# A per-pair scale made on all partitions by one matmul, in an attention stage whose written-out order is laid out anew

## The chip, the cores and the metric

The kernel runs on one core of a Trainium2 chip. The core has five engines that each work through their own queue of instructions in order: TensorE (PE; its weight loads are shown apart as PEld), VectorE (DVE), ScalarE (ACT), GpSimd (POOL) and SyncE (SP), which here only issues DMAs. They wait for each other by semaphores. The metric is the device time of one execution in microseconds (us), lower is better. Before the change the median of three runs is 683.49 us (682.04 to 684.49).

## The reference

Attention over 2 batches x 8 heads, sequence 1152, head dimension 64, with queries averaged in pairs (576 queries a head), followed by two MLPs:

```
q_pool = q.reshape(B, H, S//2, 2, D).mean(axis=3)
scores = q_pool @ k.T / sqrt(D);  scores -= scores.max(-1)
attn   = exp(scores);  attn = attn / (attn.sum(-1) + 1e-9)
x      = attn @ v                              # -> 1152 tokens x 512
h = x @ w_in;  g = max(h,0) + alpha*min(h,0);  x = g @ w_out          # 512 -> 2048 -> 512
h = x @ w_in2; g = P(h) / (Q(|h|) + 1e-6);     out = g @ w_out2       # P cubic, Q quadratic
```

All inputs are float32, and the kernel keeps nearly float32 accuracy by splitting operands into a high and a low part and adding up the products of the parts.

## The kernel before, in words

**Pairs.** The 16 heads are worked in 8 pairs p = 0..7; head n = 2p is the even and n = 2p+1 the odd head of a pair, 9 key tiles t a head, so a pair is 18 steps. For each step PE makes scores (`score`, L1049, four matmuls into an `st` tile), ACT exponentiates (`p_exp`, L1057, PSUM tile `st` to the tile `PF`), DVE or POOL forms the low part (`p_lo`, L1063, tile `PL`), and PE multiplies with V (`av`, L1075, L1077 and L1079, 15 matmuls into the accumulator tile `o` of the head, with the high and low part of V in `V16`). When a head's nine steps are done, `norm` (L1088 to L1090, DVE) divides `o` into the tile `x`.

**Beside that, for the next pair.** While pair p-1 runs its scores, PE, ACT and DVE also find the row maxima of pair p (`max_mm` L962, `max_relu` L968, `max_1` L971, `max_2` L976), and the operands of pair p+1 are prepared: `load_q` (tile `qr`), `load_k` (`kr` or `ring`) and `load_v` (`vr`) are DMAs from HBM; `q_sum` (L820, POOL, tile `qs`) adds the two query halves; `k_hi` and `q_hi` (ACT, L824 and L838, tiles `kh` and `qh`) round to the high parts; `k_diff` (L827, POOL), `q_lo` and `k_lo` (DVE) follow; and `k1_move`, `qh_move`, `ql_move`, `k2_move` (all recorded at L816, on SP) copy the parts by DMA into the matmul operands `K1`, `QQ` and `K2`. All DMAs of the kernel are issued from SP, in the order of its queue.

**V's scale.** V is scaled by a power of two per pair, from the largest |V|. `v_abs` (L889, ACT) sums |V| by partition into `am`, one number a partition. `v_max` (L899, PE) transposes this column: the stationary operand is the one column `am`, the moving one the identity, the output one row of 128 numbers in a free corner of the accumulator tile `o` of the even head then in work. `v_scale` (L904 to L909, DVE) takes the maximum of that row and forms the scale and its inverse, on one partition (tile `g`). `v_scale2` (L912, PE) spreads the two numbers over 128 partitions by a matmul with a row of ones, into the same corner of `o`, and `v_scale3` (L917, DVE) copies them to the tile `vs`. `v_hi` (L934, ACT) and `v_lo` (L938, DVE) use `vs`. Since `v_max` and `v_scale2` write the tile `o` and DVE reads it, the next `av` matmuls into `o` wait for DVE.

**What sets the order.** Every call is put into one list with a time in steps (`at(time, fn, ...)`; pair p starts at 18p), the list is sorted by time, and the instructions are issued in that order, so each engine's queue has the list's order. The number is no clock: an instruction runs when its queue has come to it and its semaphores are there. A table `NUDGE`, looked up by the function's name and its time (pairs 1 to 5 by the time within the pair), adds a correction to it.

**Late in attention** the weights of the first MLP are unpacked as well: five operations a tile on ACT, DVE (`w_shift` L657, `w_top` L662, `w_low` L670) and POOL. From then on the MLPs run as a stream of matmuls (L708 and L1331).

Of the kernel before, what the change touches and what calls it, by code (L numbers as in the profile page):

```python
# [21 lines left out]
P = 128  # L22

NUDGE = {
    "av +10.35": 0.124,
    "av +11.35": -0.146,
    "av +15.34": -0.123,
    "av +15.35": 0.109,
    "av +2.35": 0.223,
    "av +4.34": -0.294,  # L30
    "av +4.35": 0.851,
    "av +8.34": -0.854,
    "av +8.35": -0.053,
# [24 lines left out]
    "av 17.35": 1.881,
    "av 4.35": 0.449,
    "av 6.34": -0.922,  # L60
    "av 6.35": 0.509,
    "av 8.35": 0.307,
    "first_kd -51.10": 0.806,
    "first_kd -54.50": 0.086,
    "first_kh -52.00": -0.087,
    "first_kh -52.60": 0.123,
    "first_kh -55.31": 0.328,
    "first_kh -55.32": 0.122,
    "first_kh -55.80": -0.617,
    "first_kl -51.00": 1.543,  # L70
    "first_kl -53.40": -0.149,
    "first_m -48.09": 7.849,
    "first_qh -50.30": -0.541,
    "first_qh -51.00": -0.312,
    "first_qh -51.80": 0.273,
    "first_qh -53.50": -1.065,
    "first_qh -55.95": 0.245,
    "first_ql -51.10": 0.279,
    "first_ql -55.30": 0.085,
    "init_1 -59.90": -3.438,  # L80
    "init_2 -59.70": -0.534,
    "init_3 -48.10": 9.574,
    "k1_move +7.30": -0.198,
    "k1_move +9.10": 2.890,
    "k1_move -47.27": 5.618,
    "k1_move -47.90": 4.202,
    "k1_move 11.70": 2.488,
    "k1_move 13.50": 1.398,
    "k2_move +0.36": 2.161,
    "k2_move +11.50": 0.543,  # L90
    "k2_move 108.36": 1.833,
    "k2_move 15.90": -0.539,
    "k2_move 8.10": -0.649,
    "k2_move 8.20": 1.103,
    "k_diff +6.50": 0.474,
    "k_diff -47.90": 0.005,
    "k_diff 10.90": -0.273,
    "k_hi +5.50": 0.667,
    "k_hi -47.90": -1.004,
    "k_hi 9.90": 0.525,  # L100
    "k_lo +10.00": 0.415,
    "k_lo 14.40": -1.147,
    "k_lo 7.04": -0.214,
    "load_k +13.00": -0.638,
    "load_k -59.98": 3.729,
    "load_k -59.99": 0.074,
    "load_k 1.50": 0.485,
    "load_k 13.00": -0.200,
    "load_q +13.00": 5.133,
    "load_q -59.97": 0.305,  # L110
    "load_q -60.00": -2.525,
    "load_q 1.50": 0.105,
    "load_q 13.00": 3.721,
    "load_v +13.00": -0.984,
    "load_v -59.96": 2.431,
    "load_v 0.69": 0.463,
    "load_v 13.00": 1.710,
    "max_1 +0.83": -0.321,
    "max_1 +10.86": 0.076,
    "max_1 +12.30": 0.259,  # L120
    "max_1 +2.27": -0.100,
    "max_1 +3.70": 0.078,
    "max_1 +8.00": -0.159,
    "max_1 -49.55": 0.073,
    "max_1 -50.55": 0.080,
    "max_1 -51.55": -0.390,
    "max_1 -52.55": -0.144,
    "max_1 -53.55": 0.216,
    "max_1 0.55": -0.363,
    "max_1 10.50": -0.036,  # L130
    "max_1 108.83": -0.043,
    "max_1 111.70": -0.169,
    "max_1 113.13": 0.091,
    "max_1 114.56": 0.031,
    "max_1 116.00": 0.031,
    "max_1 117.43": 0.031,
    "max_1 118.86": 0.031,
    "max_1 12.80": 0.042,
    "max_1 120.30": -0.006,
    "max_1 15.10": 0.428,  # L140
    "max_1 16.25": 0.161,
    "max_1 4.22": -0.411,
    "max_1 5.44": 0.202,
    "max_1 7.05": -0.166,
    "max_1 8.20": -0.037,
    "max_1 9.35": -0.040,
# [1320 lines left out]
```

## Time and profile before

| | us |
|---|---|
| median of 3 runs | 683.49 (682.04 to 684.49) |
| profiled execution, its own time | 685.3 |
| span of the profiled execution | 681.8 |
| PE busy in the span | 646.8 (95%) |
| DVE busy | 515.9 (76%) |
| ACT busy | 484.5 (71%) |
| POOL busy | 402.7 (59%) |

The span runs from the first to the last instruction; the profiled execution's own time has a little more around it. Busy time is a mean over stages that have different limits, so what matters is which wait ends last in the stage in question: the list of waits names the engine and line that waited, and the one that released it; the timeline shows where it stood; and a table of stretches shows what the stage took. The granted clock (PEclk) is 1.00 or 0.50 of TensorE's full speed, 2.4 or 1.2 GHz.

### The profile page before, as it was taken

To read this page: it belongs to the slowest core of one execution; us is meant where nothing else is said; L and a number is where in the kernel's file an instruction comes from. 1 tells how busy PE (TensorE), PEld (TensorE's weight loads), DVE (VectorE), ACT (ScalarE), POOL (GpSimd) and SP (SyncE) were. 2 spreads that over 40 slices of the span, in tenths; PEclk is the share of its full clock that TensorE was granted. 3 is DMA by queue.
4 is the path that set the end of the run, shared out by engine and by line. 5 is a ranking of instruction groups with operands and counts; after the bars stand their busy time and mean duration, and the time that the engine had idled before them with its cause. 6 is when DMAs were issued, how large, how long until landed. Compare 5 with 4: busy or idle time off the path is not lost.

```text
span 681.8 us, 13647 instructions
## 1 busy us (share of the span) xinstructions
PE 646.8 (95%) x5194; PEld 580.2 (85%) x5194; DVE 515.9 (76%) x949; ACT 484.5 (71%) x902; POOL 402.7 (59%) x353
## 2 busy tenths in 40 slices
PE   6798999799998889999999999999998999999997
PEld 5677999798897879999999999999887779999995
DVE  8887666769677998998992149996788877767774
ACT  5666687577867756666764368888788888778774
POOL 5554677567676775676664226785466655444442
PEclk8799799899999979999999999999999999999999
DMA  4778759595684224343331005640320010001001
GB/s 173 192 203 176 156 137 212 119 230 122 168 196 114 68 92 154 126 140 138 128 133 49 1 0 189 232 167 32 124 92 32 1 47 1 2 0 48 1 0 46
DMA packets 20960, 72.28 MB, mean 106 GB/s; under 512 B 3104, under 2 KB 3104, under 8 KB 20896
## 3 DMA queue, kind: packets, MB, share of 16 engines
q1 hardware_dynamic: 20896, 71.42, 37.3%
q8 instruction: 40, 0.66, 0.4%
q14 instruction: 24, 0.20, 0.1%
HBM read 47.72 MB, written 2.36 MB: 73 GB/s over the span
## 4 chain that ended last, share of the span: by engine, by line
PE 61%; DVE 19%; ACT 9%; issue 5%; DMA 4%; SPq 1%; POOL 1%; POOLq 0%; DVEq 0%; ACTq 0%
PE hp L708 20%; PE acc L1331 18%; PE st L1049 9%; PE m L962 5%; DVE bits L662 3%; PE o L1075 3%; PE o L1077 2%; PE o L1079 2%; DVE bits L657 2%; DMA QQ<-qh 2%; DVE ring L670 2%; DMA QQ<-qs 1%; DVE g L1312 1%; DVE g L1297 1%; DVE hp L1310 1%
## 5 line engine op out<-in xcount | busy, mean ns | idle before, releaser
L1063 POOL TENSOR_TENSOR PL<-PF 128x576 f16<-128x576 f32 x106 | 132.5, 1262 | 65.2 <-ACT PF L1057 64.0
L1320 POOL TENSOR_TENSOR gl<-g,gh 128x384 fp32r<-128x384 f32 x96 | 104.7, 1091 | 72.2 <-ACT gh L1316 58.2
L1057 ACT ACTIVATE PF<-st 128x576 f32<-128x576 f32 x144 | 91.4, 651 | 41.4 <-PE st L1049 35.1
L1331 PE MATMUL acc<-woh,gl 128*128 128x512 f32 x288 | 114.4, 397 | 3.2 <-POOL gl L1320 3.2
L1331 PE MATMUL acc<-woh,gh 128*128 128x512 f32 x288 | 113.3, 393 | 2.1 <-ACT m L1362 1.7
L1331 PE MATMUL acc<-wol,gh 128*128 128x512 f32 x288 | 113.2, 393 | 0.0
L1049 PE MATMUL st<-QQ,K 128*128 128x288 f32 (+1 forms) x576 | 107.8, 314 | 0.2
L1290 POOL TENSOR_TENSOR b<-a,b 128x384 f32<-128x384 f32 x48 | 48.9, 1018 | 84.5 <-ACT b L1278 83.3
L1049 PEld LDWEIGHTS st<-QQ,K 128*128 128x128 f32 (+1 forms) x576 | 90.6, 198 | 2.5 <-ACT PF L1057 0.8
L1075 PE MATMUL o<-V,PF 128*128 128x65 f16 x720 | 80.1, 197 | 11.2 <-DVE vs L917 6.9
L708 PE MATMUL hp<-xh,wih 128*128 128x384 f32 x384 | 83.7, 340 | 0.0
L708 PE MATMUL hp<-xl,wih 128*128 128x384 f32 x384 | 83.1, 338 | 0.0
L708 PE MATMUL hp<-xh,wil 128*128 128x384 f32 x384 | 83.0, 338 | 0.0
L962 PE MATMUL m<-K,QQ 128*128 128x384 f32 x234 | 73.8, 387 | 7.8 <-DMA QQ<-qh 2.7
L1075 PEld LDWEIGHTS <-PF 128*128 128x128 bf16 x720 | 67.8, 99 | 14.0 <-DVE x L1090 5.0
L1079 PE MATMUL o<-V,PL 128*128 128x65 f16 x720 | 78.7, 195 | 0.7 <-POOL PL L1063 0.6
L1077 PE MATMUL o<-V,PF 128*128 128x64 f16 x720 | 79.3, 198 | 0.0
L708 PEld LDWEIGHTS hp<-xh,wih 128*128 128x128 f32 x384 | 69.4, 188 | 7.6
L1077 PEld LDWEIGHTS <-PF 128*128 128x128 bf16 x720 | 69.0, 100 | 6.9 <-issue 6.9
L1316 ACT ACTIVATE gh<-g 128x384 fp32r<-128x384 f32 x96 | 49.9, 520 | 31.8 <-DVE g L1281 21.8
L1079 PEld LDWEIGHTS <-PL 128*128 128x128 f16 x720 | 68.9, 101 | 0.9 <-POOL PL L1063 0.7
L1331 PEld LDWEIGHTS acc<-woh,gl 128*128 128x128 f32 x288 | 54.1, 188 | 18.1 <-POOL gl L1320 6.7
(151 smaller groups left out, 1392.1 us busy)
## 6 DMA issues: line engine op xcount, KB each, us to landing
K<-kh SPq DMA_DIRECT2D x28, 384.0 KB, 6.2
ring<-in_w SPq DMA_DIRECT2D x19, 512.0 KB, 3.5
raw<-in_w SPq DMA_DIRECT2D x13, 512.0 KB, 3.5
ring<-in_w1o SPq DMA_DIRECT2D x10, 512.0 KB, 3.4
qr<-in_qT SPq DMA_DIRECT2D x8, 576.0 KB, 9.5
vr<-in_v SPq DMA_DIRECT2D x8, 576.0 KB, 9.1
ring<-in_w2o SPq DMA_DIRECT2D x9, 512.0 KB, 3.5
QQ<-qh SPq DMA_DIRECT2D x14, 288.0 KB, 5.0
```

Source lines behind the costliest of these rows:

```text
L708: nc.tensor.matmul(hp, lhsT=w_[:, c * P:(c + 1) * P], rhs=x_[:, c, ts], start=k == 0, stop=k == 3 * KT - 1)
L962: nc.tensor.matmul(s[:, 0:CW], lhsT=of(QQ, n)[:, 0, k * P:(k + 1) * P], rhs=of(K1, n)[:, k0:k0 + CW], start=n == parts[0][0], stop=n == pa ...
L1049: nc.tensor.matmul(st[:, hf, 0:HALF], lhsT=k_[:, ks], rhs=q_[:, c:c + HALF], start=first, stop=not first)
L1057: nc.scalar.activation(out=PF[buf(n, t)][:, 0:SQ].rearrange("p (h q) -> p h q", h=2), in_=ST.pop((n, t))[:, :, 0:HALF], func=AF.Exp, scale=SC)
L1063: e.tensor_tensor(out=PL[u][:, 0:SQ], in0=PF[u][:, 0:SQ], in1=top(PF[u])[:, 0:SQ], op=ALU.subtract)
L1075: nc.tensor.matmul(o, lhsT=ph, rhs=V16[i][:, t, 0:D + 1], start=first, stop=False, skip_group_check=True)
L1077: nc.tensor.matmul(o[:, 1:D + 1], lhsT=ph, rhs=V16[i][:, t, D + 1:2 * D + 1], start=False, stop=False, skip_group_check=True)
L1079: nc.tensor.matmul(o, lhsT=pl, rhs=V16[i][:, t, 0:D + 1], start=False, stop=last, skip_group_check=True)
L1290: nc.gpsimd.tensor_tensor(out=E[u, "b"], in0=E[u, "a"], in1=E[u, "b"], op=ALU.mult)
L1316: nc.scalar.activation(out=G[u][0], in_=E[u, "g"], func=AF.Copy)
L1320: nc.gpsimd.tensor_tensor(out=gl, in0=E[u, "g"], in1=gh.bitcast(F32), op=ALU.subtract)
L1331: nc.tensor.matmul(acc, lhsT=g_[:, cs], rhs=w_, start=f == 0 and k == 0, stop=f == NF - 1 and k == 2)
```

## The change

The scale is made on all 128 partitions at once: `v_max`'s stationary operand is the column `am` repeated 128 times, so that every row of the output has the 128 numbers, and `v_scale` runs the same five DVE operations on 128 partitions, and writes `vs` itself. `v_scale2`, `v_scale3`, the row of ones and its memset are gone. The table `NUDGE` (some 510 entries) is replaced by another one of some 200, which also names a few calls of the first MLP steps; of it two lines are shown.

```
-    "load_q +13.00": 5.133,          # and some 510 more
+    "k2_move +11.50": 3.52954,       # and some 200 more
...
     def where(time, fn):
         if S2 <= time < S2 * (NP - 2):
             return f"{fn.__name__} +{time % S2:.2f}"
+        s = (time - S2 * NP - 1) / 3.3
+        for i, (a, b) in enumerate(((5, 30), (35, 46), (51, 62), (66, 92))):
+            if a <= s < b:
+                return f"{fn.__name__} {i}"
         return f"{fn.__name__} {time:.2f}"
...
-    ones1 = hold.tile([1, P], F16, name="ones1")
...
-        nc.tensor.matmul(AM[p, 1][0:1, VC:VC + P], lhsT=top(AM[p]), rhs=ident16, start=p == 0, stop=True,
-                         skip_group_check=True)
+        nc.tensor.matmul(AM[p, 1][:, VC:VC + P], lhsT=top(AM[p]).to_broadcast([P, P]), rhs=ident16,
+                         start=p == 0, stop=True, skip_group_check=True)
...
     def v_scale(p):
-        g = AM[p, 0] = small.tile([1, 8], F32, tag="g", name="g")
-        nc.vector.tensor_reduce(out=g[:, 0:1], in_=AM[p, 1][0:1, VC:VC + P], axis=AX.X, op=ALU.max)
+        g = small.tile([P, 5], F32, tag="vs", name="vs", bufs=3)
+        VS[p] = g[:, 3:5]
+        nc.vector.tensor_reduce(out=g[:, 0:1], in_=AM[p, 1][:, VC:VC + P], axis=AX.X, op=ALU.max)
...
-    def v_scale2(p):
-        nc.tensor.matmul(AM[p, 1][:, VC + P:VC + P + 2], lhsT=ones1, rhs=top(AM[p, 0])[:, 3:5], start=p == 0,
-                         stop=True, skip_group_check=True)
-
-    def v_scale3(p):
-        VS[p] = small.tile([P, 2], F32, tag="vs", name="vs", bufs=3)
-        nc.vector.tensor_copy(VS[p], AM[p, 1][:, VC + P:VC + P + 2])
-
-    def v_scale_at(t1, t2, p):
-        at(t1, v_max, p)
-        at(t1 + 0.2, v_scale, p)
-        at(t2, v_scale2, p)
-        at(t2 + 0.2, v_scale3, p)
+    def v_scale_at(time, p):
+        at(time, v_max, p)
+        at(time + 0.2, v_scale, p)
```

**The order around V's scale.** DVE's queue in the middle of pair 3 (heads 6 and 7), before: the scale's five operations on `g`, V's low part, a maximum, a low part `PL`, then the copy to `vs`.

```order
L976 ISA junk_2261,nm<-m_2259,relu 128x384
L976 ISA nm 128x1
L904 TENSOR_REDUCE g<-o 1x1
L905 TENSOR_SCALAR g<-g 1x1
L906 TENSOR_SCALAR g<-g 1x1
L908 TENSOR_SCALAR g<-g 1x1
L909 RECIPROCAL g<-g 1x1
L938 SCALAR_TENSOR_TENSOR V_1_117<-vr,vs,V_1_117 128x9x64
L971 TENSOR_REDUCE nm<-m_2284 128x1
L1063 TENSOR_TENSOR PL_124<-PF_118 128x576
L917 COPY vs<-o 128x2
```

The same place in the change (L594 to L599 are the scale, L618 V's low part):

```order
L656 ISA junk_2234,nm<-m_2228,relu 128x384
L656 ISA nm 128x1
L618 SCALAR_TENSOR_TENSOR V_1_117<-vr,vs,V_1_117 128x9x64
L594 TENSOR_REDUCE vs<-o 128x1
L595 TENSOR_SCALAR vs<-vs 128x1
L596 TENSOR_SCALAR vs<-vs 128x1
L598 TENSOR_SCALAR vs<-vs 128x1
L599 RECIPROCAL vs<-vs 128x1
L651 TENSOR_REDUCE nm<-m_2269 128x1
L656 ISA junk_2313,nm<-m_2309,relu 128x384
```

V's low part now stands ahead of the scale's reduction, and after the reduction the scale reads the tile `o` no more. PE's queue there, before, where the fifth `av` of head 6 follows the spreading matmul:

```order
L1049 MATMUL st<-QQ_108,K_01_103 128x288 x2
L1049 MATMUL st<-QQ_108,K_01_113 128x288 x2
L912 LDWEIGHTS ones_132
L912 MATMUL o<-g,ones_132 128x2
L1075 LDWEIGHTS PF_122
L1075 MATMUL o<-V_0_116,PF_122 128x65
```

and in the change, from `v_max` to the third `av` of head 6, the first one that follows it into the tile `o`:

```order
L587 LDWEIGHTS am
L587 MATMUL o<-ident_131,am 128x128
L729 MATMUL st<-QQ_108,K_01_103 128x288 x2
L729 MATMUL st<-QQ_108,K_01_113 128x288 x2
L642 MATMUL m_2266<-K_00_102,QQ_107 128x384
L642 MATMUL m_2266<-K_11_105,QQ_110 128x384
L642 MATMUL m_2269<-K_00_102,QQ_107 128x384
L642 MATMUL m_2269<-K_11_105,QQ_110 128x384
L755 LDWEIGHTS PF_120
L755 MATMUL o<-V_0_116,PF_120 128x65
```

One score and four maximum matmuls stand between `v_max` and the next user of `o`.

**The order of the DMAs.** SP's queue over the preparation of one pair (p = 5), before: moves of the even and odd head's operands, then V, a `K2` move (`K_01_113<-kr`), the next pair's K and q, and the other `K2` move.

```order
L816 DMA K_12_106<-kh 64x1536 x2
L816 DMA QQ_111<-qs 64x576
L816 DMA QQ_111<-qh 64x2x576
L816 DMA QQ_108<-qs 64x576
L816 DMA QQ_108<-qh 64x2x576
L816 DMA K_01_103<-kh 64x1536 x2
L928 DMA vr<-in_v 128x1152
L816 DMA K_01_113<-kr 64x1152
L813 DMA ring<-in_kT 128x1152
L807 DMA qr<-in_qT 128x1152
L816 DMA K_11_115<-kr 64x1152
```

The same stretch in the change:

```order
L504 DMA K_12_106<-kh 64x1536 x2
L504 DMA QQ_111<-qh 64x2x576
L504 DMA QQ_111<-qs 64x576
L504 DMA QQ_108<-qs 64x576
L504 DMA K_01_103<-kh 64x1536 x2
L504 DMA QQ_108<-qh 64x2x576
L608 DMA vr<-in_v 128x1152
L495 DMA qr<-in_qT 128x1152
L501 DMA ring<-in_kT 128x1152
L504 DMA K_01_113<-kr 64x1152
L504 DMA K_11_115<-kr 64x1152
```

The loads of q and K have moved ahead of both `K2` moves, q ahead of K. In the preparation of pair 2, the first one of this kind, the two loads for pair 3 have moved further: ahead of all the moves of pair 2 (before, K stood second and q third to last among these). On ACT, `k_hi` and the next `max_relu` now stand ahead of `q_hi`; before, `q_hi` came first.

**The order at the start.** ACT's queue from the second `max_relu` of pair 0 on, before:

```order
L968 ACTIVATE relu<-m_229 128x384
L861 ACTIVATE QQ_109<-qs 64x576 x3
L968 ACTIVATE relu<-mst 128x384
L968 ACTIVATE relu<-m_254 128x384
L824 ACTIVATE kh<-kr 128x1152
L889 ACTIVATE junk,am<-vr 128x1152
L838 ACTIVATE qh<-qs 128x576
```

and in the change:

```order
L648 ACTIVATE relu<-m_222 128x384
L577 ACTIVATE junk,am<-vr 128x1152
L549 ACTIVATE QQ_109<-qs 64x576
L648 ACTIVATE relu<-mst 128x384
L648 ACTIVATE relu<-m_253 128x384
L512 ACTIVATE kh<-kr 128x1152
L526 ACTIVATE qh<-qs 128x576
```

The sum over |V| (L889, now L577) has moved ahead of the last two `max_relu`. Of PE's eighteen warming matmuls sixteen stood ahead of the first maxima and two behind them; now it is eleven and seven. Near the end of attention, on DVE, `norm` of head 13 stands ahead of a `w_shift`, before behind it.

## Rows read from the trace of the kernel before

**Rows 1.** Stretches cut at each pair's first score: engines' busy us (instructions), granted clock, DMA.
```profile
55.30:89.20 33.90, 30.99 (x405) 28.36 (x404) 21.45 (x53) 21.62 (x41) 20.10 (x17) 0.85 0.80 167
89.20:116.10 26.90, 26.53 (x394) 24.50 (x390) 20.55 (x52) 20.86 (x39) 20.07 (x17) 1.00 0.69 164
116.10:147.60 31.50, 27.90 (x393) 25.76 (x390) 22.11 (x52) 20.83 (x39) 19.56 (x17) 0.95 0.74 162
147.60:175.30 27.70, 26.54 (x394) 24.51 (x391) 21.45 (x52) 20.87 (x40) 20.09 (x17) 1.00 0.72 171
...
202.50:233.50 31.00, 28.26 (x409) 25.02 (x406) 24.60 (x60) 22.16 (x44) 19.68 (x17) 1.00 0.39 115
233.50:259.10 25.60, 21.45 (x304) 19.71 (x301) 24.52 (x32) 15.56 (x29) 18.27 (x16) 0.87 0.23 72
259.10:660.00 400.90, 395.77 (x2059) 356.33 (x2058) 304.20 (x463) 293.63 (x551) 226.20 (x197) 1.00 0.22 78
```

**Rows 2.** Waits of PE in attention: who waited <- for whom: us, times, longest.
```profile
PE o L1075 <- DVE vs L917: 6.9, 6, 3.6
...
PE m L962 <- DMA QQ<-qh: 2.7, 1, 2.7
```

**Rows 3.** Timeline of all engines in pair 3: start, us, instruction, [idle before <- releaser].
```profile
124.27 0.22 PE L899 MATMUL o<-ident,am 128*1 128x128 f16 x1
...
124.96 0.27 DVE L904 TENSOR_REDUCE g<-o 1x1 f32<-1x128 f32 x1
...
125.71 1.41 POOL L820 TENSOR_TENSOR qs<-qr 128x576 f32<-128x576 f32 x1 [3.97 <-DMA K<-ring]
...
125.77 0.21 PE L1075 MATMUL o<-V,PF 128*128 128x65 f16 x1
...
125.88 1.86 DVE L938 SCALAR_TENSOR_TENSOR V<-vr,vs,V 128x576 f16<-128x576 f32 x1
...
127.16 0.69 ACT L838 ACTIVATE qh<-qs 128x576 fp32r<-128x576 f32 x1 [2.45 <-POOL qs L820]
...
131.34 0.15 DVE L917 COPY vs<-o 128x2 f32<-128x2 f32 x1
...
131.53 0.21 PE L1075 MATMUL o<-V,PF 128*128 128x65 f16 x1 [3.60 <-DVE vs L917]
```

**Rows 4.** Timeline of SP's DMA issues in pair 3.
```profile
109.43 1.82 SPq L928 DMA_DIRECT2D vr<-in_v  x1
...
114.58 0.49 SPq L807 DMA_DIRECT2D qr<-in_qT  x1
```

**Rows 5.** SP's issues in pair 1, and PE's timeline behind them.
```profile
53.60 0.97 SPq L807 DMA_DIRECT2D qr<-in_qT  x1
54.61 1.07 SPq L816 DMA_DIRECT2D QQ<-qh  x1
...
67.69 0.66 PE L962 MATMUL m<-K,QQ 128*128 128x384 f32 x1 [2.66 <-DMA QQ<-qh]
```

**Rows 6.** The half-clock stretch behind it, as in rows 1.
```profile
66.50:76.60 10.10, 8.66 (x78) 7.89 (x78) 3.98 (x9) 4.45 (x7) 6.45 (x6) 0.50 0.41 83
```

**Rows 7.** Single lines: count, shortest/median/longest ns (the last, of the page: busy us, mean ns).
```profile
L938 DVE SCALAR_TENSOR_TENSOR V<-vr,vs,V x16: 791/810/1864, 26.5 to 245.6; 128x576 f16<-128x576 f32 x16
...
L899 PEld LDWEIGHTS <-am x8: 78/79/80, 18.7 to 211.2; 128*1 128x1 bf16 x8
...
L1075 PEld LDWEIGHTS <-PF 128*128 128x128 bf16 x720 | 67.8, 99 | 14.0 <-DVE x L1090 5.0
```

**Rows 8.** Timeline of ACT at the start.
```profile
15.87 0.47 ACT L968 ACTIVATE relu<-m 128x384 f32<-128x384 f32 x1
...
17.43 1.15 ACT L889 ACTIVATE junk<-vr 128x1152 f16<-128x1152 f32 x1
18.48 0.19 ACT L889 ACTIVATION_READ_ACCUMULATOR junk<-vr 128x1 f32 x1
```

**Rows 9.** DVE and PE at the start of pair 7.
```profile
238.78 1.36 DVE L657 TENSOR_SCALAR m<-m 128x512 int32<-128x512 int32 x1
...
241.09 0.23 PE L1075 MATMUL o<-V,PF 128*128 128x65 f16 x1 [2.63 <-DVE x L1090]
```

More of the change, by code (lines that the diff above doesn't have):

```diff
@@ L81 @@
[L81 to L98, printed above, removed]
@@ new lines @@
+    "k1_move +9.10": 0.23557,
+    "k1_move -47.27": 10.43481,
+    "k1_move -47.90": 1.14559,
+    "k1_move 13.50": 2.06168,
+    "k2_move +11.50": 3.52954,
+    "k2_move 15.90": 0.25394,
+    "k_diff -47.90": 0.51613,
+    "k_hi +5.50": 0.25949,
+    "k_hi -47.90": -0.62568,
+    "k_hi 9.90": -0.18769,
+    "k_lo +10.00": 0.29991,
+    "k_lo 14.40": -1.12051,
+    "k_lo 7.04": 0.068,
+    "load_k 1.50": -0.45811,
+    "load_k 13.00": -2.88791,
+    "load_q 13.00": -1.62319,
+    "load_v 13.00": 1.45393,
@@ new lines @@
+    "max_relu +10.59": 0.58365,
+    "max_relu 11.38": 0.5297,
+    "max_relu 111.43": 0.06242,
+    "max_relu 120.03": 0.0309,
+    "max_rows +14.31": 0.10269,
+    "max_rows 122.31": 0.10644,
+    "max_rows 13.37": -0.51768,
+    "max_rows 6.47": -0.12553,
+    "max_split +13.18": -0.03436,
+    "max_split -48.61": 0.83619,
+    "max_split 16.84": -0.0646,
+    "mlp_consts 128.00": -1.81761,
+    "mlp_consts 133.00": -2.60458,
+    "mlp_in 145.28": 0.26062,
+    "norm 11.76": 0.08995,
+    "norm 146.76": 0.06323,
@@ new lines @@
+    "p_lo 135.05": 0.12577,
+    "p_lo 15.05": 0.351,
+    "p_lo 3.05": 1.42472,
+    "p_lo 4.05": 0.6012,
+    "p_lo 9.05": 0.07221,
+    "prelu 150.61": -0.04042,
+    "prelu 153.91": -0.17391,
+    "prelu 160.51": -0.10483,
+    "q_hi +6.40": 0.08961,
+    "q_hi -47.70": -0.48782,
+    "q_hi 10.80": 0.07506,
+    "q_lo +7.40": 0.04673,
+    "q_lo 0.57": -1.43941,
+    "q_lo 11.80": -0.12073,
+    "q_sum +5.20": -0.328,
+    "q_sum -48.20": -0.97478,
+    "q_sum 9.60": -0.52929,
+    "qh_move +9.15": 2.44673,
@@ new lines @@
+    "qh_move -47.60": -0.06471,
+    "ql_move +9.20": -0.24027,
+    "ql_move 0.57": 0.05439,
+    "ql_move 0.59": 0.34068,
+    "score +13.00": -0.03661,
+    "score +2.00": 0.21903,
+    "score 0.00": 0.035,
+    "score 109.00": -0.29656,
+    "score 112.00": -0.46662,
+    "score 119.00": 0.00873,
+    "score 120.00": 0.05223,
+    "score 131.00": -0.04076,
+    "score 132.00": 0.05883,
+    "score 135.00": -0.05311,
+    "score 16.00": -0.03369,
+    "v_abs +4.00": -0.72454,
+    "v_abs -49.53": -2.21325,
@@ new lines @@
+    "v_hi +14.96": -1.87022,
+    "v_hi 14.96": -0.13172,
+    "v_lo 15.69": 2.86818,
+    "v_max +5.40": 0.4685,
+    "v_scale +5.60": 0.37753,
+    "v_scale -47.78": 1.58608,
+    "w_abs 113.65": 0.03395,
+    "w_abs 132.54": 0.43108,
+    "w_abs 136.32": -0.14805,
+    "w_abs 140.10": -0.19452,
+    "w_abs 150.79": -0.27065,
+    "w_hi 117.58": -0.40418,
+    "w_hi 132.69": -0.03525,
+    "w_hi 154.45": 0.20359,
+    "w_lo 118.41": -0.47373,
+    "w_lo 144.86": 0.62232,
+    "w_lo 148.64": -0.65956,
@@ new lines @@
+    "w_lo 154.55": 1.08052,
+    "w_lo 160.82": 1.91379,
+    "w_load 128.37": -0.29771,
+    "w_load 156.72": -0.06508,
+    "w_load 162.99": -0.01728,
+    "w_low 116.29": -0.0647,
+    "w_low 127.63": 0.04751,
+    "w_low 131.40": -0.00732,
+    "w_low 138.96": -0.11673,
+    "w_low 153.17": 0.03283,
+    "w_low 156.30": 0.01707,
+    "w_shift 151.44": 0.67325,
+    "w_shift 163.98": 0.07386,
+    "w_top 122.70": 0.95861,
+    "w_top 130.25": -0.63679,
+    "w_top 137.81": 0.1087,
+    "w_top 141.59": -0.07738,
@@ L536 @@
+    "w_top 158.80": 0.05655,
+    "x_hi +16.29": -0.24823,
+    "x_hi 124.29": 0.04022,
+    "x_hi 142.29": 0.08267,
+    "x_hi 149.50": 0.07739,
+    "x_lo 124.69": -0.11644,
+    "x_lo 142.69": 0.14185,
+    "x_trans +15.79": 0.01432,
+    "x_trans 141.79": -2.01456,
+    "x_trans 149.00": -0.06218,
 }
```

581 lines of the change are left out of this document (87 added, 494 removed).

## The prediction, made before the changed kernel ran

> **What bounds the kernel now.** I read the table of stretches first, cut at each pair's first score [rows 1]. From 259.1 us on the MLPs keep PE busy for 395.8 of 400.9 us, and apart from their first steps the change leaves them alone: what it does is decided in the first 259 us. There the reader is to see that pairs with the same work take different times. The pair at 89.2 took 26.9 us with PE busy for 26.5 of them, which is what a pair costs when PE hardly waits. The one at 55.3 took 33.9 us, 7.0 more, the one at 116.1 31.5, 4.6 more, and the one at 147.6 27.7, 0.8 more; PE's instruction counts in them differ by 3% at most. In the last pair before the MLPs (233.5 to 259.1) PE works for 21.5 of 25.6 us and DVE for 24.5: that pair is DVE's.
>
> The list of waits says what PE waited for [rows 2]: 6.9 us in six `av` for the copy of V's scale (L917), and 2.7 us once for the query's high part in `QQ`. The timeline of all engines then shows the longest of the six [rows 3]. At 131.53 `av` had waited 3.60 us for the copy at 131.34. The copy takes 0.15 us, but stands in DVE's queue behind a low part `PL`, that one behind an exponential of ACT, and ACT had itself stood 2.45 us ahead of `q_hi` at 127.16, waiting for POOL's `q_sum`, which started at 125.71 after 3.97 us without work. Its input q had been issued at 114.58, last but one of its chain and 5.1 us behind the load of V at 109.43 [rows 4]. So a late load of q travels through POOL, ACT and DVE to PE, because the scale's copy ties `av` to DVE's queue. The other long wait has the same kind of cause: at 67.69 PE had waited 2.66 us for a `QQ` move that SP issued at 54.61, right behind a load of q for a later pair [rows 5].
>
> Both waits cost twice. Behind the first, PE's granted clock was 0.50 from 66.5 to 76.6 (1.2 instead of 2.4 GHz) [rows 6], and the two long pairs have mean clocks of 0.85 and 0.95, the undisturbed ones 1.00 [rows 1]. PE had been idle for over 2.5 us before the clock fell; the pair at 147.6, whose waits were short, kept it.
>
> **The change part by part**, against the profiled execution's own 685.3 us (span 681.8 and 3.5 around it).
>
> *The scale itself.* Eight spreading matmuls and eight DVE copies go. DVE's eight copies are 8 x 0.15 [rows 3] = 1.2 us of DVE time, in six pairs beside PE's work and worth nothing there. The matmuls, short and pipelined, I estimate at 0.1 us of PE's issue each: -0.8. The five DVE operations keep their length, since a row of 128 numbers is as long on 128 partitions as on one (bound: 0 to 0.1 us each, off PE's path). The weight load of `v_max` goes from one column (79 ns) to 128; the nearest row, `av`'s load of 128 columns, has 99 ns [rows 7]: 8 x 0.02 = +0.16. The Trainium skill (TensorE: Matmul & The Clock Gate, LDWEIGHTS) has the load grow with the columns, columns/1.2 ns: 107 ns against one, which would be an estimated +0.85 us. The rows do not bear out so large a step, for the one-column load already takes 79 ns. Sum: -0.65.
>
> *The waits for the copy.* The 3.60 belongs to the pair at 116.1 and another 0.25 to the half-clock stretch; the remaining four are 6.9 - 3.6 - 0.25 = 3.05 us. With no copy, `av` has nothing to wait for there; after the wait the next thing late could be `PL` from POOL, so I take -2.4 (0 to -3.05).
>
> *The pair at 116.1.* With q ahead of K and of both `K2` moves, q goes out directly behind V, some 3 us earlier, and the two transfers between go behind it; that is about the 3.97 us that POOL stood. `k_hi` and `max_relu` no longer stand behind `q_hi`. The pair should come near 26.9: -4.3 of the 4.6 (-1 to -4.6).
>
> *The pair at 55.3.* The move that PE waited for now stands ahead of V and of two `K1` moves, but both loads for pair 3 stand ahead of all moves of pair 2. The last operand of the odd head is then late by less, I judge, if at all: -5.0 of 7.0 (0 to -7.0), the clock's part included. Against it, the even head's operands get a load of q put ahead of them, whose issue took 0.97 us at 53.60 [rows 5], and they are wanted soon after 55.3. I take that 0.97 as a wait: +1.0 (0 to +2.7, the one wait for such a move [rows 2]).
>
> *A wait that comes anew.* `v_max` still writes `o`, DVE's reduction still reads it, and the third `av` must wait for that. Before, the reduction at 124.96 stood ahead of V's low part, and `av` came at 125.77, undisturbed. Now V's low part stands first. It takes 0.81 us in the median and 1.86 at worst [rows 7]. With 0.81 the reduction would end at about 124.96 + 0.81 + 0.27 = 126.04, a wait of 0.3; with 1.86, 1.3 us. If the maximum ahead of it is ready earlier, as its matmul now stands ahead of an `av`, the wait is 0. Seven times 0 to 1.3; I take 0.25 each: +1.7. Behind `av` on PE only the next maximum and score queue, and ACT waits for these.
>
> *The start.* The sum over |V| takes 1.15 us and its readout 0.19 [rows 8]. It ran at 17.43, and with the `QQ` copy that goes with it now stands ahead of two ReLUs, the later of which ran at 15.87. The maxima, the first row of scores and the first moves shift by about that much. Against it, five more warming matmuls just ahead may have the clock up sooner. I take +0.9 (-1 to +1.5, all of the 1.34 and a little).
>
> *The end of attention.* `norm` ahead of `w_shift` (1.36 us) takes that much off the 2.63 us that PE waited at 241.09 [rows 9], and the half clock behind it (mean 0.87 there [rows 1]) should shorten. But DVE has little room: -1.0 (+1.5 to -2.6).
>
> Sum: -0.65 - 2.4 - 4.3 - 5.0 + 1.0 + 1.7 + 0.9 - 1.0 = -9.75. 685.3 - 9.8 = 675.5; that execution lies 1.8 above the median, and against 683.5 it is **673.7 us**.
>
> **Rivals.** *Only the scale's own waits go.* Nearly every order is new, and each of the 2 to 3 us stalls that go could come back at another place: the start, the even head's operands, V. Then 3.05 and 0.65 remain, and part of the long pairs: -2 to -6, about 679.5. For it speaks that the stalls came of moves being a few us late, which can't be seen in an order; against it that q, at the root of one, is now early.
>
> *Nothing to be measured.* The DVE-bound end and the new wait take back what the middle gives: two waits of 1.3 in each of four pairs would be 10 us. 683.5 +- 2. Against it: in most pairs V's low part has its short length.
>
> *Slower, by the reduction behind V's low part.* If V's low part meets POOL's work each time, it takes 1.86, as at 125.88 where POOL's `q_sum` ran from 125.71 [rows 3]; and if DVE is late by another 1.3, PE waits over 2.6 us in each of seven pairs, the length behind which the clock fell. At 2.6 + 1.0 of clock (the pair at 116.1 was 4.6 longer for a wait of 3.6), 7 x 3.6 = +25.2 us against -11.4 from the other terms: about 697. It decides the sign from 1.6 us a pair on. For it: V's low part now always stands between. Against: median 0.81. The Trainium skill (SBUF — State Buffer, SBUF: two separate sides) says that VectorE with two SBUF inputs and GpSimd take their shared ports as an exclusive lock, the loser standing for the whole instruction. The 1.86 us beside POOL's 1.41 us agree with it; by that rule every meeting costs DVE the rest of a POOL instruction, and the reduction then pays it too.
>
> **How the numbers follow.** Forecast (-6 to -17): 0.64. More than that: 0.02. Scale's waits only: 0.20. Nothing: 0.08. Slower: 0.06. A change of 0.3%, 2 us, is about what a measurement of this kernel can tell from none. Faster is 0.64 + 0.02 + 0.20 = 0.86, same 0.08, slower 0.06. The range: the lower end takes most of the terms near their better bounds (-17.5: 666); the upper end takes in most of the second case (-2: 681.5).
>
> **What the profile after would show.** Right: no wait of `av` for a copy; POOL's `q_sum` and ACT's `q_hi` without idle time ahead of them; pairs at 55, 89, 116 and 147 within a us of 27; clock 1.00 through the middle; a first score some 1 us later. Wrong, by step: `av` waiting for the scale's reduction (new wait); maxima waiting for `K1` or `QQ` moves in the pair at 55; a half-clock stretch in any middle pair; MLPs that begin less than 6 us earlier than 259.

## The result, and the profile after

The changed kernel's median is 675.04 us (674.37 to 677.09, 4 runs) against 683.24 (682.04 to 684.49, 4 runs) of the kernel before: a ratio of 0.9885, 95% interval 0.9856 to 0.9913. The profiled execution took 675.5 us of its own time with a span of 673.7. The forecast was 673.7, in a range of 666.0 to 681.5.

That agrees to 1.3 us, but not for the reasons of the sum. The table of stretches, cut again within 0.2 us of each pair's first score (columns as in [rows 1]), shows it; its first line is the first pair of the kernel before, the others are the changed kernel's:

```profile
21.10:55.30 34.20, 31.52 (x344) 26.41 (x342) 28.24 (x71) 23.56 (x44) 17.23 (x16) 0.94 0.90 222
```

```profile
21.70:63.50 41.80, 35.79 (x358) 32.06 (x356) 27.73 (x70) 23.50 (x46) 17.85 (x16) 0.76 0.91 224
63.50:90.00 26.50, 26.30 (x387) 24.22 (x385) 21.36 (x52) 21.42 (x41) 20.24 (x17) 1.00 0.58 130
...
116.50:142.90 26.40, 26.23 (x391) 24.24 (x388) 20.63 (x51) 20.68 (x40) 20.62 (x17) 1.00 0.77 184
...
195.90:224.80 28.90, 26.53 (x392) 24.18 (x389) 24.71 (x56) 21.73 (x43) 20.40 (x17) 1.00 0.33 95
224.80:252.40 27.60, 22.52 (x356) 20.45 (x353) 27.28 (x36) 18.05 (x34) 21.20 (x17) 0.94 0.30 97
252.40:673.70 421.30, 411.84 (x2110) 369.13 (x2106) 313.09 (x480) 304.08 (x569) 231.84 (x203) 1.00 0.21 75
```

The five pairs from 63.5 to 195.9 (two are shown) all take 26.4 to 26.5 us at full clock, where they had taken 33.9, 26.9, 31.5, 27.7 and 27.2: PE hardly waits there any more. The pair behind them takes 28.9 instead of 31.0. But the first pair, which no term of the sum spoke of, takes 41.8, where it took 34.2 before (its first score stood at 21.1, the next pair's at 55.3).

In the middle the chain of [rows 3] is gone. The timeline of SP, POOL, PE, DVE and ACT in the pair at 116.5 (lines have moved: `load_q` is L495, `q_sum` L508, `q_hi` L526, V's low part L618, the reduction L594, `av` L755):

```profile
112.72 1.08 SPq L495 DMA_DIRECT2D qr<-in_qT  x1
...
122.20 1.42 POOL L508 TENSOR_TENSOR qs<-qr 128x576 f32<-128x576 f32 x1
...
124.60 0.22 PE L587 MATMUL o<-ident,am 128*128 128x128 f16 x1
...
125.10 0.81 DVE L618 SCALAR_TENSOR_TENSOR V<-vr,vs,V 128x576 f16<-128x576 f32 x1
...
125.84 0.27 DVE L594 TENSOR_REDUCE vs<-o 128x1 f32<-128x128 f32 x1
...
126.16 0.19 PE L755 MATMUL o<-V,PF 128*128 128x65 f16 x1
...
126.49 0.73 ACT L526 ACTIVATE qh<-qs 128x576 fp32r<-128x576 f32 x1
```

No row carries an idle time: q went out directly behind V, so `q_sum` (3.97 us of idle POOL before) and `q_hi` (2.45 of ACT) wait for nothing. The load was issued 3.9 us ahead of its pair's first score instead of 1.5, and it also landed sooner, 7.16 us after its issue instead of 10.97 [rows 4]. The reduction ends at 126.11 and `av` comes at 126.16, undelayed.

The first pair is another matter. PE's waits in it, in the timeline, and its clock behind them in two stretches of the table:

```profile
32.49 0.44 PE L688 MATMUL mtp<-ident,mt 128*2 128x128 f16 x5 [0.84 <-DVE mt L674]
...
35.19 0.98 PE L642 MATMUL m<-K,QQ 128*128 128x384 f32 x2 [1.69 <-issue]
...
39.23 0.69 PE L642 MATMUL m<-K,QQ 128*128 128x384 f32 x1 [1.14 <-DVE nm L656]
...
52.26 0.72 PE L688 MATMUL mtp<-ident,mt 128*2 128x128 f16 x5 [2.12 <-DVE mt L674]
```

```profile
35.00:45.00 10.00, 8.67 (x54) 7.82 (x55) 4.76 (x10) 4.50 (x9) 4.31 (x3) 0.50 0.71 204
52.00:58.00 6.00, 5.74 (x47) 5.04 (x48) 3.59 (x8) 1.83 (x4) 0.00 (x0) 0.50 0.99 217
```

PE is busy for 35.8 of the 41.8 us, against 31.5 of 34.2: 3.3 us more of waits and 4.3 more of busy time, at a mean clock of 0.76 instead of 0.94 (and with 358 matmuls recorded there instead of 344).

### The profile page after: what moved, and what is told of

It is laid out like the page before. It is cut to its first block, busy times and chain, and to the rows that moved or that the text cites. A ratio compares the mean times of both kernels' runs of the same rounds, so it can differ in the third digit from the quotient of the medians.

```text
span 673.7 us, 13635 instructions
## 1 busy us (share of the span) xinstructions
PE 641.8 (95%) x5186; PEld 578.5 (86%) x5186; DVE 513.9 (76%) x941; ACT 484.3 (72%) x902; POOL 408.2 (61%) x352
## 4 chain that ended last, share of the span: by engine, by line
PE 59%; DVE 24%; ACT 8%; issue 6%; DMA 1%; POOL 1%; POOLq 0%; DVEq 0%; SPq 0%; ACTq 0%
PE hp L398 20%; PE acc L1011 19%; PE st L729 8%; PE m L642 5%; DVE bits L352 3%; PE o L755 2%; DVE PL L743 2%; PE o L757 2%; PE o L759 2%; DVE ring L360 2%; DVE bits L347 2%; DVE junk L656 2%; DVE g L992 1%; ACT junk L577 1%; DVE g L977 1%
## 5 line engine op out<-in xcount | busy, mean ns | idle before, releaser
L743 POOL TENSOR_TENSOR PL<-PF 128x576 f16<-128x576 f32 x106 | 140.2, 1336 | 65.0 <-ACT PF L737 61.7
L729 PE MATMUL st<-QQ,K 128*128 128x288 f32 (+1 forms) x576 | 106.4, 313 | 0.6 <-ACT PF L737 0.6
L755 PE MATMUL o<-V,PF 128*128 128x65 f16 x720 | 78.5, 196 | 2.7 <-DVE x L770 1.4
L759 PE MATMUL o<-V,PL 128*128 128x65 f16 x720 | 77.1, 193 | 3.2 <-DVE PL L743 2.7
L757 PE MATMUL o<-V,PF 128*128 128x64 f16 x720 | 77.7, 197 | 0.0
L755 PEld LDWEIGHTS <-PF 128*128 128x128 bf16 x720 | 67.1, 98 | 10.6 <-issue 2.7
L757 PEld LDWEIGHTS <-PF 128*128 128x128 bf16 x720 | 68.1, 99 | 1.8 <-issue 1.4
```

The lines of the kernel that those rows point to most:

```text
L729: nc.tensor.matmul(st[:, hf, 0:HALF], lhsT=k_[:, ks], rhs=q_[:, c:c + HALF], start=first, stop=not first)
L743: e.tensor_tensor(out=PL[u][:, 0:SQ], in0=PF[u][:, 0:SQ], in1=top(PF[u])[:, 0:SQ], op=ALU.subtract)
L755: nc.tensor.matmul(o, lhsT=ph, rhs=V16[i][:, t, 0:D + 1], start=first, stop=False, skip_group_check=True)
L757: nc.tensor.matmul(o[:, 1:D + 1], lhsT=ph, rhs=V16[i][:, t, D + 1:2 * D + 1], start=False, stop=False, skip_group_check=True)
L759: nc.tensor.matmul(o, lhsT=pl, rhs=V16[i][:, t, 0:D + 1], start=False, stop=last, skip_group_check=True)
```

## The experiments

All ran beside the kernel before on their chip, whose median was 681.25 us beside scale_only, order_only, q_early and start_before, 682.05 beside init_before, pair0_before and warm_fill, and 681.09 beside the rest (17, 11 and 18 runs, from 677.5 to 686.6); ratios are to these. Line numbers in rows are each kernel's own.

| run | median us | ratio to before (95%) |
|---|---|---|
| scale_only | 681.02 | 0.9987 (0.9960 to 1.0014) |
| order_only | 675.76 | 0.9897 (0.9870 to 0.9924) |
| q_early | 675.96 | 0.9902 (0.9874 to 0.9931) |
| q_scale | 674.62 | 0.9911 (0.9875 to 0.9946) |
| q_late | 682.38 | 1.0028 (1.0002 to 1.0054) |
| init_before | 674.81 | 0.9895 (0.9866 to 0.9923) |
| pair0_before | 673.99 | 0.9881 (0.9857 to 0.9906) |
| start_before | 671.36 | 0.9834 (0.9806 to 0.9862) |
| rows_late | 675.48 | 0.9917 (0.9885 to 0.9948) |
| warm_fill | 674.98 | 0.9905 (0.9879 to 0.9931) |
| spliced_warm | 672.03 | 0.9869 (0.9832 to 0.9905) |

### Which of the two edits: scale_only and order_only

scale_only is the kernel before with the scale's edit alone, its table untouched:

```
-            v_scale_at(k - 12.598, k - 10.836, p)
+            v_scale_at(k - 12.598, p)          # v_max and v_scale as in the change
```

> The kernel before with its table as it was, and the scale made on all partitions (no spreading matmul, no copy). Theory (the order brings the gain, the scale's own edit little): the copy waits go, 6.9 us in six, but the pair at 116 still has its late q and waits there for a low part PL instead, so 679.5 to 682. Rival (tying av to DVE's queue through the copy was the whole matter): all of the copy waits and the half clock behind the 3.6 go, pairs at 116 and 147 at 27 us or less, and the time is 675 to 677, with no need of a new order.

No difference that can be told. The waits for the copy are gone, and the late q makes others of them, as the timeline of the pair at 113.8 shows:

```profile
122.78 1.42 POOL L818 TENSOR_TENSOR qs<-qr 128x576 f32<-128x576 f32 x1 [3.36 <-DMA qr<-in_qT]
...
124.23 0.69 ACT L836 ACTIVATE qh<-qs 128x576 fp32r<-128x576 f32 x1 [1.85 <-POOL qs L818]
...
126.99 1.51 DVE L1053 TENSOR_TENSOR PL<-PF 128x576 f16<-128x576 f32 x1 [1.71 <-POOL PL L1053]
...
129.04 0.44 PE L952 MATMUL m<-K,QQ 128*128 128x384 f32 x1 [1.30 <-DVE nm L966]
```

POOL and ACT stand for q as in [rows 3], and PE waits, now a maximum for DVE in place of `av` for the copy. The pair takes 30.4 us, and the other pairs from the second to the sixth take 28.2 to 28.5. The theory holds, the rival falls; but PE waits there longer for the maximum (1.30) than for the low part `PL` (0.52) that was expected.

order_only is the changed kernel with the old scale put back, at its old times:

```
-            v_scale_at(k - 12.598, p)
+            v_scale_at(k - 12.598, k - 10.836, p)     # with v_scale2 and v_scale3
```

> The changed kernel with its new order, and the scale made on one partition and spread and copied as in the kernel before. Theory (the order brings the gain): with q early nothing in front of the copy is late, av's waits for the copy are under 1 us each, the pairs from the second to the sixth stay within 1 us of 26.5, and the time is 675.5 to 678. Rival (the scale's edit brings it): av waits 2 us or more for the copy in several pairs, the clock falls behind them, 681 to 686.

675.76: as the theory had it. Its pairs from the second to the sixth take 26.7 to 26.8 us, against 26.5 with the scale's edit: by these two profiles some 0.25 us a pair is what that edit is worth under the new table. Its first pair takes 39.0 us, 2.8 less than the change's; why was not tested.

### The place of one load: q_early, q_late, q_scale

q_early is the kernel before with one entry of its table changed:

```
-    "load_q +13.00": 5.133,
+    "load_q +13.00": -0.97,
```

> The kernel before with one entry changed: from pair 4 on the load of q stands directly behind the load of V, ahead of two moves and the load of K. Theory (the late q travels through POOL, ACT and DVE to av): POOL's 3.97, ACT's 2.45 and av's 3.60 us in the pair at 116 fall to under 1 each, that pair takes 27 to 28 us, 678.5 to 680.5. Rival (the copy is late for another reason, such as DVE's own queue): av still waits over 2 us there, 682 to 684.

675.96 us, 2.5 below the best that was expected, 2.0 of which are the kernel before itself (681.25 here, 683.24 where the expectation came from). The stretch of the pair that had taken 31.5 us, and its timeline:

```profile
112.10:139.00 26.90, 26.55 (x394) 24.51 (x391) 20.55 (x54) 20.88 (x40) 20.05 (x17) 1.00 0.79 187
```

```profile
117.93 1.42 POOL L820 TENSOR_TENSOR qs<-qr 128x576 f32<-128x576 f32 x1
...
120.80 0.72 ACT L838 ACTIVATE qh<-qs 128x576 fp32r<-128x576 f32 x1
...
124.32 0.15 DVE L917 COPY vs<-o 128x2 f32<-128x2 f32 x1
...
124.52 0.19 PE L1075 MATMUL o<-V,PF 128*128 128x65 f16 x1 [0.35 <-DVE vs L917]
```

POOL and ACT wait for nothing, and `av`'s wait for the copy, which is still there, is 0.35 instead of 3.60. The four pairs from 85 to 193 us take 26.9 each. The pair at 55 is the check: the load of q that falls into it was not moved, and there `av` still waits for the copy:

```profile
70.75 0.19 PE L1075 MATMUL o<-V,PF 128*128 128x65 f16 x1 [2.07 <-DVE vs L917]
```

q_late turns it round: the changed kernel, whose table has no entry for that load, with the load put back where it stood:

```
+    "load_q +13.00": 3.7,
```

> The changed kernel with the load of q from pair 4 on put back behind the load of K and one K2 move, as it stood before. Theory (q's place is the gain in the middle, and av or the maxima then wait for what stands behind q_hi, copy or no copy): pairs from the third to the sixth at 27 to 29.5 us and 677 to 682. Rival (the new order or the scale without a copy bears a late q): those pairs within 0.3 of 26.5, 674.5 to 676.5.

682.38: with q late again, all of the change's gain is gone. In the profiled execution, a long one of 686.15 us, the four pairs from the third to the sixth take 28.5 to 28.9 us, the second, whose load stays early, 26.5. Of the pair at 119.5 the stretch, and the timeline where V's scale is made:

```profile
119.50:148.00 28.50, 26.54 (x394) 24.32 (x391) 22.54 (x51) 20.77 (x40) 20.71 (x17) 1.00 0.74 171
```

```profile
127.42 1.43 POOL L509 TENSOR_TENSOR qs<-qr 128x576 f32<-128x576 f32 x1 [2.11 <-DMA K<-ring]
127.97 1.50 DVE L619 SCALAR_TENSOR_TENSOR V<-vr,vs,V 128x576 f16<-128x576 f32 x1
...
129.39 0.28 DVE L595 TENSOR_REDUCE vs<-o 128x1 f32<-128x128 f32 x1
...
129.72 0.19 PE L756 MATMUL o<-V,PF 128*128 128x65 f16 x1 [0.55 <-DVE vs L595]
```

A late `q_sum` runs beside V's low part, which takes 1.50 instead of 0.81, and `av` waits for the reduction behind it. That is the slower rival of the prediction, in place. The list of waits of this kernel sums it up (who waited <- for whom: us, times, longest):

```profile
PE m L643 <- DVE nm L652: 5.6, 6, 1.3
PE o L756 <- DVE vs L595: 4.0, 5, 1.1
```

q_scale is scale_only with the entry of q_early, so the kernel before with two edits:

```
-            v_scale_at(k - 12.598, k - 10.836, p)
+            v_scale_at(k - 12.598, p)
...
-    "load_q +13.00": 5.133,
+    "load_q +13.00": -0.97,
```

> The kernel before with two edits: the scale made on all partitions, and the load of q directly behind that of V from pair 4 on. Theory (the two gains add: q takes the late chain away, the scale's edit the 0.37 us waits for the copy and its PE and DVE time): pairs from the third to the sixth at 26.5 us, 673.5 to 675.3. Rival (with q early the scale's edit is worth nothing that can be told): 675.4 to 677, pairs at 26.9.

674.62 lies in the theory's range, but its reason fails: the pairs take 27.1 us, not 26.5. In place of the 0.35 for the copy, a maximum waits 0.75 for DVE. The intervals of q_early, q_scale and the full change overlap.

### The same kernel twice: before_again

> The kernel before, unchanged, profiled once more. Theory (the 2.66 us for QQ in the pair at 55.3 came from transfers that were late in that one execution, since the kernel with only q moved, which has the same program up to then, waited 0.54 there): the wait at about 67 us is under 1.5 us or of another size, the pair at 55 takes 29.5 to 32 us, and the 3.6 us in the pair at 116 is back within 0.5. Rival (both waits belong to the order): 2.66 and 3.6 come back within 0.3, and the pair at 55 takes 33.9 again.

This execution took 678.05 us, less than each of before's runs on that chip (679.29 to 685.05). Its stretches and waits for the two pairs that had been 33.9 and 31.5:

```profile
55.10:85.90 30.80, 28.85 (x400) 26.35 (x400) 23.00 (x52) 21.63 (x42) 20.75 (x17) 0.94 0.81 180
113.30:141.30 28.00, 26.54 (x395) 24.51 (x392) 21.18 (x53) 20.98 (x40) 19.85 (x17) 1.00 0.74 179
```

```profile
69.98 0.19 PE L1075 MATMUL o<-V,PF 128*128 128x65 f16 x1 [1.84 <-DVE vs L917]
...
126.97 0.19 PE L1075 MATMUL o<-V,PF 128*128 128x65 f16 x1 [1.46 <-DVE vs L917]
```

The wait for `QQ` did not come back, and the 3.60 was 1.46: the theory holds for the first and misses the second, which varies as well. One thing that differs is how long the loads of q took, here the profile's lines on them in the first and in this execution (count, KB, median us from issue to landing):

```profile
qr<-in_qT SPq DMA_DIRECT2D x8, 576.0 KB, 9.5
```

```profile
qr<-in_qT SPq DMA_DIRECT2D x8, 576.0 KB, 7.9
```

The load of q that ends in the 3.60 and the 1.46 landed 10.97 us after its issue in the first execution and 8.09 in this one. Why the transfers differ is not shown.

### The first pair: init_before, pair0_before, start_before, rows_late, warm_fill, spliced_warm

The first three take table entries of the kernel before into the changed one: those with times under 0 (init_before, 61 of them), those from 0 to 18 (pair0_before, 154), or both (start_before). Two of the entries:

```
-    "v_abs -49.53": -2.21325,
+    "v_abs -49.53": 0.752,
...
-    "norm 11.76": 0.08995,
+    "norm 11.76": 1.381,
```

> The changed kernel with the entries before the first score (times under 0) of the kernel before. Theory (the start's order costs the most: first moves at 20.95 against 19.51 us, V's sum ahead of the maxima): the first pair comes to 36 to 38 us, 671 to 672.5. Rival (the entries of the first pair itself cost it): 674.5 to 676.

> The changed kernel with the entries of the first pair (times 0 to 18) of the kernel before, and its own start. Theory (the start's order costs the most): the first pair stays at 39 to 42 us, 674 to 676. Rival (the entries of the first pair itself cost it): it comes to 36 to 37 us, 671 to 672.5.

The first pair in init_before, and in pair0_before:

```profile
21.50:63.00 41.50, 35.64 (x357) 32.53 (x356) 27.49 (x70) 23.41 (x43) 18.88 (x17) 0.76 0.91 226
```

```profile
21.90:56.60 34.70, 30.38 (x338) 25.36 (x337) 27.68 (x70) 23.11 (x45) 16.25 (x15) 0.97 0.90 220
```

My theory (the start) fell: the entries of the first pair itself cost it 7 us. The time, 673.99, is still 1.5 to 3 above what the rival expected; in the profile the second pair took 29.0 us (26.5 in the changed kernel) and the last 29.8 (27.6).

> The changed kernel with the table entries of the start and of the first pair (times under 18) of the kernel before. Theory (the first pair's 41.8 us after, against 34.2, are the new start order's waits and half clock, and nothing was moved out of later pairs for them): the first pair takes 34 to 36 us, the second to sixth stay at 26.5 to 27.5, 667 to 669. Rival (the first pair took over what the second waited for before): the second pair goes back to 31 to 34 us, 673 to 677.

671.36 us, the fastest of all, and its interval lies wholly below that of order_only, which ran beside it. It falls between the theory's 667 to 669 and the rival's 673 to 677: the first pair took 35.9, as the theory had it, but the second 28.5, so 2.0 of 5.8 us came back there. That it beats pair0_before by 2.6 is in the profiles mostly the last pair (27.5 against 29.8), which these entries don't touch; the last section comes to it.

rows_late moves one group of the first pair, five transposes, behind a score and an `av` step, with the `max_put` that follows it:

```
-    "max_put 13.64": -0.64861,
+    "max_put 13.64": -0.218,
...
-    "max_rows 13.37": -0.51768,
+    "max_rows 13.37": -0.183,
```

> The changed kernel with one group of five PE transposes of the first pair's stretch (max_rows of pair 1) behind a score and an av step instead of ahead of them, where the table before had them. Theory (they stood ahead of the work that could have covered their chain of ACT and DVE, 2.12 us of idle PE and half clock from 52 to 58 us): that wait falls under 0.7, no half clock there, the first pair takes 37 to 39.5 us, 671 to 673.5. Rival (the next maxima and scores wait for the same chain or for moves anyway): another wait of 1.5 to 2 us comes up before 63 us, 674.3 to 676.

The rival was right: the first pair takes 42.4 us, the 2.12 us stays, and only its place changes, to a maximum's matmul that waits for the same line of DVE:

```profile
PE m L642 <- DVE mt L674: 2.1, 1, 2.1
```

warm_fill adds 20 warming matmuls ahead of the first `v_max`, since PE stood idle at 17.9 us:

```
-        (1.375, warm, 11), (11.256, warm, 5), (12.01, warm, 2),
+        (1.375, warm, 11), (11.256, warm, 5), (12.01, warm, 22),
```

> The changed kernel with 20 more warming matmuls ahead of the first v_max, where PE then stood idle for 2.85 us. Theory (PE's clock falls behind that idle time, and PE's own pace sets the first scores): the clock stays 1.00 from 20 to 25 us, the first pair is 1 to 2.5 us shorter than 41.7, 673 to 674.5. Rival (the first pair waits for its moves, which start at the same time): the clock holds, but the waits at 33 to 38 and 50 us grow by as much, 675 +- 0.7.

674.98, no difference. The clock stayed 1.00 from 20 to 25 us and the first pair became 2 us shorter, as the theory had it, but the first score came 1.15 us later, and the last pair was longer by 2.3 (last section). The time is the rival's; the two are not told apart. spliced_warm does the same in start_before, with the first `norm` earlier:

```
-        (1.375, warm, 11), (11.256, warm, 5), (12.01, warm, 2),
+        (1.375, warm, 11), (11.256, warm, 5), (12.01, warm, 22),
...
-    "norm 11.76": 1.381,
+    "norm 11.76": 0.2,
```

> The kernel with the entries of the start and first pair of before (671.36), with 20 more warming matmuls ahead of the first v_max, and the first norm moved earlier. Theory (half clock from 17 to 28 and 48 to 52 us there came behind idle times of 2.96 and 0.90, and PE's pace sets the first pair): clock 1.00 in both, first pair 33 to 34.5 us, 668.5 to 670. Rival (the first pair waits for its moves, DMA share 0.90 there): the same waits a little later, 671 to 672.

672.03 against 671.36: nothing gained. The first pair shrank to 32.0 us at full clock, and the second one grew, for its moves were not there yet:

```profile
23.10:55.10 32.00, 29.47 (x343) 24.61 (x342) 28.73 (x73) 23.84 (x46) 16.94 (x15) 1.00 0.90 227
55.10:87.80 32.70, 29.37 (x400) 27.00 (x398) 21.79 (x52) 21.61 (x41) 19.69 (x17) 0.90 0.81 177
```

```profile
PE m L775 <- DMA QQ<-qh: 3.2, 1, 3.2
```

That is the rival: with DMA 0.90 busy in the first pair, PE stood 3.2 us in the second for a move, and the second's mean clock was 0.90. Which of the first pair's entries cost the 7 us is left open.

## Why the prediction was right in its number, and where its steps failed

By stretches of the two profiled executions: the start +0.6, the first pair +7.6, then -7.4, -0.4, -5.1, -1.2, -0.7 and -2.1, the last pair up to the first MLP matmul +0.4 (27.2 before, from 233.5 to 260.7), the MLPs +0.2: -8.1 in the span, and 1.7 less around it (3.5 before, 1.8 after). That is -9.8, and the sum said -9.75. The exactness is luck: against the 7.6 of the first pair and the 1.4 by which the end missed its term stand 3.4 beyond the terms of the pair at 55, 0.8 at 116, some 3 in the four other pairs and the 1.7 outside the span.

**The pair at 116 (-4.3; measured -5.1): right in cause and path, the size in part that execution's.** q_early and q_late show the cause from both sides: the load's place alone makes the pair 26.9, and takes it back to 28.5. But the kernel before took only 28.0 there in before_again, so 3.5 of the 5.1 belonged to the one profiled execution. What the term left out is that the same load makes the other three middle pairs late too, by less. In the medians it weighs as much as the whole change: q_early alone has 0.9902, the change 0.9885, and without it q_late has 1.0028. The rest of the change is not nothing by that; in the profiles its losses (the first pair) and its gains (the pairs at 55 and 202) come near to cancelling.

**The waits for the copy (-2.4).** The pairs at 89, 147 and 175 lost 2.3 us and the one at 202 lost 2.1, more than the term; the cause was put wrong. With q early and the copy still there, the pairs at 147 and 175 lose 0.8 and 0.3 in q_early as well; the copy's own waits are the remaining 0.35 each. The pair at 202 is neither's: it takes 30.8 in q_early, 30.9 in scale_only and 30.6 in q_scale, and 29.2 in order_only, which has the copy and the new table. So other entries of the table shortened it; which, was not tested. The rival that only the scale's waits go had it the wrong way round: scale_only gained nothing.

**The pair at 55 (-5.0, +1.0; measured -7.4).** Too small, but the same kernel took 30.8 us there in before_again, so 3.1 of it belonged to the profiled execution, in which the wait for `QQ` stood. A wait for a DMA was read as a property of the order, and in the second execution it was not there. Of the other 4.3, 2.0 came back when the first pair got its old entries again (start_before, 28.5).

**The wait that comes anew (+1.7; measured 0 six times, 0.9 once).** The step counted what DVE does, and not what PE has to do in between: a score and four matmuls of a maximum, from 124.63 to 126.1, cover the 0.81 and 0.27. The list of waits after has one row of it:

```profile
PE o L755 <- DVE vs L594: 0.9, 1, 0.9
```

The slower rival's mechanism is real all the same, as q_late shows (five waits, 4.0 us). What keeps it away is that an early q takes `q_sum` away from V's low part, which in the changed kernel hardly ever meets it (shortest, median, longest ns):

```profile
L618 DVE SCALAR_TENSOR_TENSOR V<-vr,vs,V x16: 808/816/1183, 26.1 to 236.6; 128x576 f16<-128x576 f32 x16
```

**The scale itself (-0.65).** No run shows the 0.1 us of a spreading matmul by itself. scale_only without these matmuls and copies is not faster, and order_only with them takes some 0.25 us more a pair, waits included. The weight load of 128 equal columns was bounded well, a median of 96 ns against 79 [rows 7]:

```profile
L587 PEld LDWEIGHTS <-am x8: 95/96/146, 17.4 to 204.0; 128*128 128x128 bf16 x8
```

The Trainium skill (TensorE: Matmul & The Clock Gate, LDWEIGHTS) has columns/1.2 ns, by which 128 columns would take an estimated 107 ns. The trace does not agree on the step from 1 to 128 columns: it is 17 ns.

**The start (+0.9; measured +0.6): right** in size, with the clock at 1.00 up to 21.2 us, where it had been 0.50 from 11.8 to 25.5.

**The first pair (no term; measured +7.6): the step that failed.** The prediction took the pairs one by one from the second on and left the first out, as though its table entries were not replaced too. pair0_before shows that it is these entries: with the old ones the pair takes 34.7. A view was at hand that raises the question, PE's order from 21 to 55 us of both kernels and what each maximum then waits for; whether it would have given the 7 us is not shown.

**The end (-1.0; measured +0.4).** The wait for `norm` went from 2.63 to 1.35 us, as the term had it, but three waits for a low part `PL` of DVE came up, 2.7 us together. It was not tested apart; the last section has one of the three.

**The clock.** "PE had been idle for over 2.5 us before the clock fell" holds for the pair at 116 (0.50 from 131.3, PE idle from 127.9) and was misread for the one at 55. The wait of 2.66 us ended at 67.69 [rows 5] and so began at 65.03, and the clock is at 0.50 from 66.5 [rows 6]: PE had then been idle for some 1.5 us, and the rest of the wait came behind the fall. In the changed kernel the clock is at 0.50 from 34.9 us, behind idle times of 0.84 and of 1.69, the second not yet over. The 2.6 us that the slower rival asked for rests on that reading.

## What to carry to other kernels

When a wait names a small copy, follow the chain past it: here it ran through DVE, ACT and POOL to one load in SP's queue, and moving that load by two places gave what taking away the copy did not. Go through every stretch whose order changes, also those where the profile before shows no trouble, for a good place there can be lost. And take a second profile of the kernel before when a term rests on a transfer's lateness: two executions of one program differed by 3 us in each of two pairs.

## What was not expected of the hardware

Some hundredths of a us decide a whole us. The changed kernel's last pair took 27.6 us in its profile and 29.9 in rows_late's, with the same order of instructions there. The timelines of the changed kernel, and of rows_late:

```profile
241.60 1.77 POOL L743 TENSOR_TENSOR PL<-PF 128x576 f16<-128x576 f32 x1 [1.12 <-ACT PF L737]
241.62 0.74 DVE L743 TENSOR_TENSOR PL<-PF 128x576 f16<-128x576 f32 x1
...
242.42 0.20 PE L759 MATMUL o<-V,PL 128*128 128x65 f16 x1 [0.63 <-DVE PL L743]
```

```profile
241.60 1.15 POOL L743 TENSOR_TENSOR PL<-PF 128x576 f16<-128x576 f32 x1 [1.10 <-ACT PF L737]
241.64 1.72 DVE L743 TENSOR_TENSOR PL<-PF 128x576 f16<-128x576 f32 x1
...
243.42 0.24 PE L759 MATMUL o<-V,PL 128*128 128x65 f16 x1 [1.61 <-DVE PL L743]
```

Where DVE starts 0.02 us behind POOL, it takes 0.74 and POOL 1.77; where it starts 0.04 behind, it takes 1.72 and POOL 1.15, and PE waits 1.0 us longer. With the rest of the 2.3 us goes a longer half clock, from 243.1 to 246.5 in the changed kernel and to 249.9 in rows_late; here is one stretch of both (columns as in [rows 1]):

```profile
247.00:248.00 1.00, 1.00 (x27) 0.92 (x23) 1.00 (x2) 0.89 (x2) 1.00 (x1) 1.00 0.01 4
```

```profile
247.00:248.00 1.00, 1.00 (x6) 1.00 (x5) 1.00 (x3) 0.51 (x1) 0.00 (x0) 0.50 0.01 4
```

Other profiles have such a race in the last pair too. Where DVE started 0.01 to 0.03 us behind POOL (the change, q_late, scale_only, before), it took 0.74 or 0.75; where it started 0.04 to 0.08 behind (pair0_before, rows_late, order_only, spliced_warm, before_again, warm_fill), it took 1.69 to 1.72. The kernel before stands on both sides, with 0.75 in one execution and 1.70 in the other, at no cost to PE there. The Trainium skill (SBUF — State Buffer, SBUF: two separate sides) says that one of the two, whichever starts first, holds their shared ports for a whole instruction, and that the other stands. Both timelines agree on the standing: the loser takes 0.6 to 1.0 us more, most of what the winner takes. On who wins they do not: POOL's start comes first in both.

Of the profiled kernels with the new order of the last pair, five (order_only, warm_fill, pair0_before, rows_late, spliced_warm) had the long wait and four (init_before, start_before, q_late and the change) the short one. The last pair took 28.5 to 29.9 us in the five, and 27.5 or 27.6 in the four but for q_late, whose half clock was long too (28.5). In the profiles that is most of the distance between pair0_before and start_before; how much of the scatter between runs of one kernel comes of it is not shown.
